# Attention into a mixture of experts on one core: first loads put on other queues and in another order, and one VectorE step ordered behind a copy

## The chip, the core and the metric

The kernel runs on one core of one Trainium2 chip. The metric is the device time of one launch in microseconds (us), as the median of several runs. A profile is one more execution, recorded instruction by instruction; its clock starts with the first instruction. Engines are written as the profile has them: PE (TensorE's matmuls) and PEld (its weight loads), DVE (VectorE), ACT (ScalarE), POOL (GpSimd) and SP (SyncE). A "q" behind a name (ACTq, SPq) marks work of that engine's sequencer, above all the issuing of DMAs.

## What is computed

Two stages follow each other. Attention has 8 batches, 8 heads, 576 positions and 64 values a head; heads 0 to 3 see a window of 32 positions, heads 4 to 7 every fourth position of a window of 128. Its output, 4608 rows of 512, goes into a layer of 8 experts, where each row is sent to the one expert with the highest score:

```python
scores = where(masks, q @ k.T / sqrt(D), -1e9)
attn = exp(scores - max); attn /= attn.sum() + 1e-9
x = (attn @ v) reshaped to (4608, 512)
expert = argmax(x @ w_gate); gate = softmax(x @ w_gate)[expert]
y = relu(x @ w1[expert]) @ w2[expert]        # 512 -> 1024 -> 512
out = gate * y
```

All is float32 outside; inside, only the masks are bf16.

## The kernel before, in words

**Attention** (`attention`, L487) is cut into 32 units: for each batch `b`, first the dilated heads (`ty` 1), then the plain ones (`ty` 0), each in two pairs of heads (`hl` 0 and 1). I number them u0 to u31. A unit goes through these steps, and the loop over `i` (L502) works on several units at once:

- `load_qk` (L265) and `load_v` (L289) bring q, k and v of one batch and type; each tile has one buffer, so that a load waits until the tile's last reader is through. For the first batch, `ty` 1 is loaded in two halves, one for each pair of heads.
- `turn` (L319) transposes q and k of a unit on PE (L338 for `ty` 0, L347 for `ty` 1). DVE copies q out of PSUM (L328) and ACT copies k (L330).
- `front` (L364) makes the scores on PE (L384). In batches 0 to 3 the mask is added on PE too (L372) and DVE finds the row maxima in PSUM (L400); later DVE adds the mask (L406) and then finds them (L413).
- `exponentials` (L417) runs ten ACT instructions, which also sum the rows into `den` (L421).
- `norm` (L431) belongs to the unit before: DVE adds a constant to `den` (L433), takes the reciprocal (L435), and POOL multiplies (L436).
- `weights` (L440), two steps behind, transposes on PE (L446); DVE copies (L448).
- `summed` (L452), three steps behind, multiplies by v (L461); ACT copies (L475, L482). `row_part` (L554) and `logit_part` (L570) make the rows for the experts and their scores.

When a batch is done, `route` (L583) and `tables` (L674) choose experts on DVE, POOL scatters the rows into a DRAM table `bucket` (L239), and the experts' slots become known.

**The experts** (`moe`, L1156) run in 35 or so slots of 128 rows. For each slot, `fetch` (L1132) loads the rows (L1087) and four weight blocks of 1 MB (L1106) on SP's queue. `across` (L1159) transposes the rows on PE (L1162), and DVE copies them to SBUF (L1164). Then come 64 matmuls for the first layer (L1230) and 16 for the second (L1262).

**What sets the order.** The program is written as one stream in which attention's steps and the slots' matmuls are interleaved by costs written into the code (`run_slots`, L1309). A scheduler then sets the order of instructions on each engine from readiness as it estimates it; on the chip each engine takes its instructions in that fixed order. `tc.issue_after(x)` makes an instruction stand behind `x`. The DMAs stand in the order of the queue that issues them.

At the start the queues hold this:

- SP: q of batch 0, `ty` 1 (8 DMAs, L283), q `ty` 0 (4, L270), v `ty` 1 (13, L308), v `ty` 0 (5, L292 and L295), the write of `blank` into `bucket` (L499), then q and k of batch 1, `ty` 1 (4 and 4, L278).
- ACT: the identity matrix (L186), k of batch 0, `ty` 1 (8, L283), k `ty` 0 (4, L270); behind these the ACT table load and the first copies of k.
- POOL: two mask tables (L208); after the first multiplication of `norm`, `w_gate` (L511), the packed constants `cst` (L514) and the third mask table; then `rows <- cst` (L559).

Of the kernel before, what the change touches and what calls it, by code (L numbers as in the profile page):

```python
# [16 lines left out]
OP = mybir.AluOpType  # L17
# [6 lines left out]
N, DM, E, F = B * S, H * DH, 8, 1024  # L24
# [11 lines left out]
CAP = N  # L36
# [23 lines left out]
NROWS = E * CAP + 128  # L60
# [103 lines left out]
def kernel(  # L164
# [10 lines left out]
    nc = tc.nc  # L175
    packed, at, exact, mask_at, packed_last, last_at = _constants()
    bucket = nc.dram_tensor("bucket", (NROWS, ROW), F32, kind="Internal").ap()
# [20 lines left out]
    blank = cpool.tile([128, ROW], F32, name="blank")  # L198
# [8 lines left out]
    def load_masks(i):  # L207
        nc.gpsimd.dma_start(masks[i], nc.inline_tensor(exact[i], name=f"c_mask{i}").ap())  # L208
# [11 lines left out]
    def wrote_bucket(i, b):  # L220


        i = getattr(i, "ins", i)
        tc.declare_no_dep(i, group="bucket", reason="no row is written twice")
        tc.add_to_no_dep_group("bucket", i)
        tc.declare_no_dep(i, group="reads", reason="rows read are full and not written again")
        bucket_writes.append((b, i))
# [22 lines left out]
    def bank(name, *dims):  # L250
        return psum.tile([128, *(dims or (512,))], F32, tag="bank", name=name)
# [5 lines left out]

    t, turns = {}, []  # L260


    STRIPS = ((0, 0, 0, 0, 96), (1, 0, 0, 96, 48), (1, 48, 1, 0, 48), (2, 0, 1, 48, 96))

    def load_qk(b, ty):  # L265
        for name, src, queue in (("q", q, nc.sync), ("k", k, nc.sync if b else nc.scalar)):
            if ty == 0:
                x = pool.tile([QT, S // QT, 4, DH], F32, tag=name + "0", name=f"{name}0_{b}", bufs=1)
                for h in range(4):
                    queue.dma_start(x[:, :, h, :], src[b, h].rearrange("(t p) d -> p t d", p=QT))  # L270
            else:


                x = pool.tile([96, 4, 3, 128], F32, tag=name + "1", name=f"{name}1_{b}", bufs=1)
                a = src[b, 4:8].rearrange("h (t m a) d -> m t h (a d)", m=2, a=2)
                for i, p0, m, t0, n in STRIPS:
                    if b:
                        queue.dma_start(x[p0 : p0 + n, :, i], a[m, t0 : t0 + n])  # L278

                for hl in () if b else range(2):  # L280
                    h = slice(2 * hl, 2 * hl + 2)
                    for i, p0, m, t0, n in STRIPS:
                        queue.dma_start(x[p0 : p0 + n, h, i], a[m, t0 : t0 + n, h])  # L283
            t[b, name, ty] = x

    def first_key(j):
        return max(0, 64 * j - WIN)

    def load_v(b, ty):  # L289
        if ty == 0:  # L290
            x = pool.tile([96, 4, 9, DH], F32, tag="v0", name=f"v0_{b}", bufs=1)
            nc.sync.dma_start(x[:, :, 0, :], v[b, 0:4, 0:96, :].rearrange("h p d -> p h d"))  # L292
            for h in range(4):
                a = v[b, h, 64 - WIN : 160 - WIN, :]
                nc.sync.dma_start(  # L295
                    x[:, h, 1:9, :],
                    bass.AP(a.tensor, a.offset, [[DH, 96], [64 * DH, 8], [1, DH]]),
                )
        else:
            x = pool.tile([96, 2, 9, 2 * DH], F32, tag="v1", name=f"v1_{b}", bufs=1)  # L300
            for j in range(9):
                lo, end = first_key(j), first_key(j) + 96
                while lo < end:
                    hi = min(end, (lo // STRIP + 1) * STRIP)
                    h, m, at0 = lo // (2 * STRIP), lo // STRIP % 2, lo % STRIP
                    a = v[b, 4 + h : 5 + h, DIL * at0 + 2 * m : DIL * at0 + 2 * m + 1, :]
                    p0 = lo - first_key(j)
                    nc.sync.dma_start(  # L308
                        x[p0 : p0 + hi - lo, :, j, :],
                        bass.AP(  # L310
                            a.tensor,
                            a.offset,
                            [[DIL * DH, hi - lo], [2 * S * DH, 2], [1, 2 * DH]],
                        ),
                    )
                    lo = hi
        t[b, "v", ty] = x
# [112 lines left out]

    def norm(e, den):  # L431

        nc.vector.tensor_scalar(den, den, 1e-9, None, op0=OP.add)  # L433
        rec = pool.tile([128, 9], F32, tag="rec", name="rec", bufs=3)
        nc.vector.reciprocal(rec, den)  # L435
        return nc.gpsimd.tensor_tensor(  # L436
            out=e, in0=e, in1=rec.unsqueeze(2).broadcast_to([128, 9, 96]), op=OP.mult
        )
# [48 lines left out]
    def attention():  # L487

        units = [(b, ty, hl) for b in range(B) for ty in (1, 0) for hl in range(2)]
        load_masks(0)
        for ty in (1, 0):
            load_qk(0, ty)
        load_masks(1)
        for ty in (1, 0):
            load_v(0, ty)

        wrote_bucket(nc.sync.dma_start(bucket[E * CAP : NROWS], blank), 0)  # L499
        qT = {n: turn(0, 1, 0, n) for n in "qk"}  # L500
        evs, dens, eTs, xTs = {}, {}, {}, {}
        for i in range(len(units) + LAG + 3):  # L502


            ended = None
            if 0 < i <= len(units):
                product = norm(evs[i - 1], dens.pop(i - 1))
                if i == 1:

                    with tc.issue_after(product.ins):  # L510
                        nc.gpsimd.dma_start(  # L511
                            wg[:, :, 0:E], moe_w_gate.rearrange("(c p) e -> p c e", p=128)
                        )
                        nc.gpsimd.dma_start(cst, nc.inline_tensor(packed, name="c_pack").ap())  # L514
                        load_masks(2)
            if i < len(units):
                evs[i], lo, places = front(qT["q"], qT["k"], units[i][1], units[i][0] < EARLY)
            u = i - LAG - 1
            if 0 <= u < len(units):
                b2, ty2, hl2 = units[u]  # L520
                xTs[u] = pool.tile([128, S], F32, tag="xT", name="xT", bufs=3)
                for part in range(2):
                    summed(eTs[u], b2, xTs[u], ty2, hl2, part)
                del eTs[u]
                if hl2 == 1 and b2 + 1 < B:
                    load_v(b2 + 1, ty2)
            if 0 <= u - 1 < len(units):
                b2, ty2, hl2 = units[u - 1]
                logit_part(b2, 2 * ty2 + hl2, xTs.pop(u - 1))
                ended = b2 if (ty2, hl2) == (0, 1) else None  # L530
            yield 3.0, ended

            if 0 <= i - LAG < len(units):
                eTs[i - LAG] = weights(evs.pop(i - LAG))
                yield 1.1, None
            if i + 1 < len(units):
                b2, ty2, hl2 = units[i + 1]
                qT = {}
                for n in "qk":
                    qT[n] = turn(b2, ty2, hl2, n)  # L540
                    yield 0.5, None
                if hl2 == 1 and b2 + 1 < B:
                    load_qk(b2 + 1, ty2)
            if 0 <= u < len(units):
                b2, ty2, hl2 = units[u]
                row_part(b2, 2 * ty2 + hl2, xTs[u])
                yield 0.55, None

            if i < len(units):
                dens[i] = exponentials(evs[i], lo, places)  # L550
# [19 lines left out]
    def logit_part(b, c, xT):  # L570


        for j, t0, n, at0 in [(j, TT * j, TT, 0) for j in range(NT - 1)] + [(0, S - REST, REST, TT)]:
            nc.tensor.matmul(  # L574
                logits[b][32 * j : 32 * j + 32, at0 : at0 + n],
                lhsT=wg[:, c],
                rhs=xT[:, t0 : t0 + n],

                start=c == 2 and at0 == 0,
                stop=c == 1 and (at0 > 0 or j > 0),  # L580
            )
# [529 lines left out]
    for j in range(NSLOT):  # L1111
        x = (j, "x", 0, 2 * j - 2)
# [43 lines left out]
    def moe():  # L1156


        def across(j):  # L1159
            ps = bank("xt", 4, 128)  # L1160
            for c in range(4):
                nc.tensor.transpose(ps[:, c], xs[j][:, 128 * c : 128 * c + 128], ident)  # L1162
            xt = mpool.tile([128, 4, 128], F32, tag="xt", name="xt")
            nc.vector.tensor_copy(xt, ps)  # L1164
            return xt

        late, xt = [], None
        for j in range(NSLOT):
# [11 lines left out]
            x = xs[j]  # L1180
            if xt is None:
                xt = across(j)
                yield 0.5
            h = mpool.tile([128, 8, 128], F32, tag="h", name="h")
# [108 lines left out]
            xt = nxt  # L1293
# [91 lines left out]
```

## Time and profile before

| What | Value |
|---|---|
| Median of 3 runs | 837.66 us (837.44 to 840.22) |
| The profiled execution: its own time | 781.94 us |
| The profiled execution: span from first to last instruction | 780.1 us |
| PE busy | 745.3 us, 96% of the span |
| PEld, DVE, ACT, POOL busy | 71%, 35%, 29%, 18% |
| Mean granted TensorE clock | 0.983 of full |
| Moved by DMA | 195.42 MB |

The profiled execution is shorter than the runs that are timed without a profile; a difference of two kernels is therefore worked out inside one profile and then set against the median. In a timeline each row is a start, a duration, an engine, a line, an operation, and the tiles (output, arrow, inputs); rows that follow each other on an engine are merged, and the bracket at the end tells how long the engine sat idle before and what ended that. In a table of windows, each row is a stretch of the span with the busy time of each engine, the granted TensorE clock and the DMA engines' share and rate. In a list of waits, each row names the waiting engine and line, what it waited for, the sum, the times, and the longest.

### The profile page before, as it was taken

The page shows a single profiled execution, that of the slowest core. Times are in us where ns is not written, and L with a number is a line of the kernel's source. Part 1 is how long each engine was busy: PE and PEld are TensorE (multiplying, and loading weights), DVE is VectorE, ACT ScalarE, POOL GpSimd, SP SyncE. Part 2 cuts the span into 40 slices and gives each one's busy share as a digit, 9 for nine tenths or more (in the row PEclk, how much of TensorE's full clock was granted, in tenths as well). Part 3 has the DMA queues.
Part 4 walks back from the last instruction along what each step waited for, and adds up shares of the span by engine and source line. Part 5 has one row for each costly group of instructions (what it writes and reads, how often), then busy time and mean ns, then how long its engine had stood idle before and what let it go on. Part 6 is the DMA issues. An engine that isn't in the chain of part 4 may idle for free.

```text
span 780.1 us, 18140 instructions
## 1 busy us (share of the span) xinstructions
PE 745.3 (96%) x6870; PEld 557.5 (71%) x6870; DVE 275.6 (35%) x963; ACT 228.9 (29%) x853; POOL 141.1 (18%) x134
## 2 busy tenths in 40 slices
PE   6798996999999999999999999999999999999993
PEld 4587875887777777777777776776776483686781
DVE  3567785755443433452241410280010111011010
ACT  3787874663333333223331100100100100100100
POOL 0414351313211310131110200160000000000000
PEclk9899998999999999999999999999999999999997
DMA  7965779999899998888317838999981683984996
GB/s 186 210 162 153 197 210 303 292 296 304 249 327 323 312 330 241 291 311 307 93 46 233 255 141 299 326 354 378 317 301 32 205 306 134 335 273 137 319 324 211
DMA packets 179644, 195.42 MB, mean 250 GB/s; under 512 B 73552, under 2 KB 105952, under 8 KB 179554
## 3 DMA queue, kind: packets, MB, share of 16 engines
q1 hardware_dynamic: 166960, 169.01, 68.8%
q0 software_dynamic: 6832, 20.54, 7.0%
q10 hardware_dynamic: 5762, 4.67, 2.0%
q8 instruction: 57, 0.93, 0.5%
q14 instruction: 33, 0.27, 0.1%
HBM read 216.16 MB, written 21.54 MB: 305 GB/s over the span
## 4 chain that ended last, share of the span: by engine, by line
PE 84%; ACT 5%; DVE 4%; issue 2%; DMA 2%; another core or an unknown queue 1%; SPq 0%; POOLq 0%; POOL 0%; ACTq 0%; DVEq 0%
PE ph L1230 32%; PE py L1262 29%; PE xo L461 4%; ACT e L421 4%; PE scores L384 3%; PE weights L446 3%; PE xt L1162 2%; PE ph L1192 2%; PE py L1192 2%; PE xrow L564 2%; PE turned L347 1%; PE turned L338 1%; PE logits L574 1%; DMA k<-in_k_dram 1%
## 5 line engine op out<-in xcount | busy, mean ns | idle before, releaser
L1230 PE MATMUL ph<-xt,w 128*128 128x128 f32 x2240 | 269.3, 276 | 4.9 <-DVE xt L1164 4.9
L1230 PEld LDWEIGHTS ph<-xt,w 128*128 128x128 f32 x2240 | 260.6, 192 | 18.6 <-issue 12.4
L1262 PE MATMUL py<-w,h 128*128 128x512 f32 x560 | 254.9, 596 | 0.0
L1262 PEld LDWEIGHTS py<-w,h 128*128 128x128 f32 x560 | 100.4, 190 | 98.1 <-issue 96.4
L1279 POOL DMA_INDIRECT out_dram<-y,to x35 | 34.7, 992 | 373.3 <-ACT y L1273 311.6
L1164 DVE COPY xt<-xt 128x512 f32<-128x512 f32 x38 | 26.2, 690 | 179.5 <-PE xt L1162 179.4
L1273 ACT ACTIVATE y<-py,x 128x512 f32<-128x512 f32 x35 | 24.0, 687 | 208.9 <-PE py L1262 161.7
L436 POOL TENSOR_TENSOR e<-e,rec 128x864 f32<-128x864 f32 x32 | 52.3, 1633 | 130.6 <-DVE rec L435 112.1
L448 DVE COPY eT<-weights 96x384 f32<-96x384 f32 x96 | 47.5, 545 | 33.0 <-PE weights L446 32.7
L421 ACT ACTIVATE e<-e,lo 128x96 f32<-128x96 f32 x144 | 51.8, 361 | 15.3 <-DVE lo L413 15.3
L421 ACT ACTIVATE e<-scores,lo 128x96 f32<-128x96 f32 (+1 forms) x160 | 52.6, 346 | 10.8 <-DVE lo L400 10.5
L239 POOL DMA_INDIRECT bucket<-rows,idx x40 | 39.1, 977 | 64.1 <-DVE idx L662 47.5
L1250 DVE TENSOR_SCALAR h<-ph 128x512 f32<-128x512 f32 x35 | 24.1, 689 | 71.4 <-PE ph L1230 71.3
L330 ACT COPY kT<-turned 128x288 f32<-128x288 f32 x64 | 22.5, 406 | 77.6 <-PE turned L338 40.3
L1241 ACT ACTIVATE h<-ph 128x512 f32<-128x512 f32 x35 | 20.8, 595 | 81.3 <-PE ph L1230 75.8
L461 PE MATMUL xo<-eT,v 96*64 96x64 f32 (+1 forms) x1216 | 44.3, 228 | 0.2 <-ACT kT L330 0.2
L461 PEld LDWEIGHTS xo<-eT,v 96*64 96x64 f32 x1216 | 39.8, 141 | 5.2 <-issue 1.1
L446 PE MATMUL weights<-ident,e 128*96 128x128 f32 x288 | 37.8, 277 | 1.8 <-POOL e L436 1.8
L384 PEld LDWEIGHTS scores<-kT,qT 64*64 64x64 f32 x1152 | 32.1, 143 | 10.0 <-issue 3.8
L384 PE MATMUL scores<-kT,qT 64*64 64x96 f32 x1152 | 37.5, 262 | 1.2 <-ACT kT L330 1.0
L446 PEld LDWEIGHTS weights<-ident,e 128*96 128x96 f32 x288 | 31.8, 128 | 8.2 <-issue 4.8
L421 ACT ACTIVATION_READ_ACCUMULATOR e<-scores,lo 128x1 f32 (+1 forms) x160 | 33.5, 210 | 0.0
(218 smaller groups left out, 592.0 us busy)
## 6 DMA issues: line engine op xcount, KB each, us to landing
w<-in_moe_w_dram SPq DMA_DIRECT2D x164, 1024.0 KB
x<-bucket SPq DMA_DIRECT2D x26, 257.0 KB
v<-in_v_dram SPq DMA_DIRECT2D x32, 192.0 KB
q<-in_q_dram SPq DMA_DIRECT2D x32, 144.0 KB
v<-in_v_dram SPq DMA_DIRECT2D x48, 96.0 KB
k<-in_k_dram SPq DMA_DIRECT2D x28, 144.0 KB
x<-bucket ACTq DMA_DIRECT2D x11, 257.0 KB
q<-in_q_dram SPq DMA_DIRECT2D x14, 192.0 KB
```

What stands on the lines that cost most here:

```text
L239: nc.gpsimd.indirect_dma_start(out=bucket, out_offset=bass.IndirectOffsetOnAxis(ap=idx, axis=0), in_=rows, in_offset=None, bounds_check=NR ...
L384: nc.tensor.matmul(sc[r][64 * c : 64 * c + 64, 96 * (i % 5) : 96 * (i % 5) + 96], lhsT=qT[rows, 64 * j : 64 * j + 64], rhs=kT[rows, first_ ...
L421: nc.scalar.activation(out=e[p0:p1, i], in_=s[:, 96 * (i - i0) : 96 * (i - i0) + 96], func=AF.Exp, bias=lo[p0:p1, i : i + 1], scale=-1.0, ...
L436: return nc.gpsimd.tensor_tensor(out=e, in0=e, in1=rec.unsqueeze(2).broadcast_to([128, 9, 96]), op=OP.mult)
L446: nc.tensor.transpose(tp[0:96, 128 * i : 128 * i + 128], e[:, a + i], ident)
L448: nc.vector.tensor_copy(eT, tp[0:96, 0:384])
L461: nc.tensor.matmul(xo[DH * h : DH * h + DH, at0 : at0 + nq], lhsT=vt[:, 2 * hl + r, j, :] if ty == 0 else vt[:, hl, j, DH * r : DH * r + D ...
L1164: nc.vector.tensor_copy(xt, ps)
L1192: nc.tensor.matmul(out[mine], lhsT=lhsT[:, mine], rhs=ws[:, (j + (g >= KIND[mixed[j]])) % 2, c, cols], start=c == 0, stop=c == n - 1,)
L1230: nc.tensor.matmul(ph[:, fi], lhsT=w1[:, c, 128 * f : 128 * f + 128], rhs=xt[:, c], start=c == 0, stop=c == 3,)
L1262: nc.tensor.matmul(py, lhsT=h[:, f], rhs=w2[:, f], start=f == 0, stop=f == 7)
L1279: i = nc.gpsimd.indirect_dma_start(out=out, out_offset=bass.IndirectOffsetOnAxis(ap=to, axis=0), in_=y, in_offset=None, bounds_check=N - 1 ...
```

## The change

Three things are changed.

First, of batch 0's k, ACT's queue keeps only the four DMAs of the first pair of heads (`ty` 1, `hl` 0). The other eight (four for the second pair, four for `ty` 0) are issued by POOL, between and behind the two mask tables.

Second, on SP's queue only v of `ty` 1 stays ahead of batch 1's q and k; v of `ty` 0 and the write of `blank` come behind these.

Third, `norm`'s first DVE instruction is ordered behind the latest copy `xt` of a slot's transposed rows that stands before it in the program. Before the first slot there is no such copy, so the order binds nothing there.

```diff
-        for name, src, queue in (("q", q, nc.sync), ("k", k, nc.sync if b else nc.scalar)):
+        for name, src in (("q", q), ("k", k)):
+            queue = nc.sync if b or name == "q" else nc.gpsimd
...
-                        queue.dma_start(x[p0 : p0 + n, h, i], a[m, t0 : t0 + n, h])
+                        (nc.scalar if (name, hl) == ("k", 0) else queue).dma_start(
+                            x[p0 : p0 + n, h, i], a[m, t0 : t0 + n, h]
+                        )
...
-        nc.vector.tensor_scalar(den, den, 1e-9, None, op0=OP.add)
+        with ExitStack() as order:
+            if crossed:
+                order.enter_context(tc.issue_after(crossed[-1].ins))
+            nc.vector.tensor_scalar(den, den, 1e-9, None, op0=OP.add)
...
         load_masks(0)
-        for ty in (1, 0):
-            load_qk(0, ty)
+        load_qk(0, 1)
         load_masks(1)
-        for ty in (1, 0):
-            load_v(0, ty)
-        wrote_bucket(nc.sync.dma_start(bucket[E * CAP : NROWS], blank), 0)
+        load_qk(0, 0)
+        load_v(0, 1)
         qT = {n: turn(0, 1, 0, n) for n in "qk"}
...
                 if hl2 == 1 and b2 + 1 < B:
                     load_qk(b2 + 1, ty2)
+                if i == 0:
+                    load_v(0, 0)
+                    wrote_bucket(nc.sync.dma_start(bucket[E * CAP : NROWS], blank), 0)
...
-            nc.vector.tensor_copy(xt, ps)
+            crossed.append(nc.vector.tensor_copy(xt, ps))
```

More of the change, by code (lines that the diff above doesn't have):

```diff
@@ L251, in bank @@
         return psum.tile([128, *(dims or (512,))], F32, tag="bank", name=name)
-    t, turns = {}, []
+    t, turns, crossed = {}, [], []
     STRIPS = ((0, 0, 0, 0, 96), (1, 0, 0, 96, 48), (1, 48, 1, 0, 48), (2, 0, 1, 48, 96))
     def load_qk(b, ty):
-        for name, src, queue in (("q", q, nc.sync), ("k", k, nc.sync if b else nc.scalar)):
+        for name, src in (("q", q), ("k", k)):
+            queue = nc.sync if b or name == "q" else nc.gpsimd
             if ty == 0:
```

## The prediction

> **What bounds the kernel now.** I read the page's busy shares first (PE 96%), then tables of windows, the list of PE's waits, and timelines of the two places where PE waits. The windows show where PE is not full: from 240 us to 760 us every stretch of 20 us has 20.00 us of PE, while the first 240 us hold 217.53, and nearly all that is missing lies before 130. So the end is set by how early PE becomes full, and only the first 130 us can give anything. PE's waits there, the three longest:
>
> ```profile
> PE turned L347 <- DMA q<-in_q_dram: 5.4, 3, 3.2
> PE ph L1230 <- DVE xt L1164: 4.9, 1, 4.9
> PE turned L347 <- ACT xT L482: 2.5, 2, 1.9
> ```
>
> The first row is loads of q: 3.2 us before the first at the start, 0.4 in the start's further loads, 1.8 for batch 1. The second is one wait in front of the first slot. The start, from its timeline:
>
> ```profile
> 1.16 6.82 ACTq L283 DMA_DIRECT2D k<-in_k_dram  x8
> 8.17 2.43 ACTq L270 DMA_DIRECT2D k<-in_k_dram  x4
> 10.62 1.28 ACT L330 ACT_TABLE_LOAD   x1 [10.62 <-DMA k<-in_k_dram]
> 11.92 1.31 ACT L330 COPY kT<-turned 128x288 f32<-128x288 f32 x4
> 12.37 1.71 PE L384 MATMUL scores<-kT,qT 64*64 64x96 f32 x34
> 22.70 2.68 SPq L278 DMA_DIRECT2D q<-in_q_dram  x4
> ```
>
> ACT issues 12 loads of k until 10.60; only then come its table load, the copies of k, and the first scores at 12.37. The last row: batch 1's q is issued at 22.70, behind v. What this costs stands in the windows (stretch, its length, busy time of PE, PEld, DVE, ACT, POOL, PE clock, DMA share, GB/s):
>
> ```profile
> 30.00:32.00 2.00, 0.32 (x4) 0.32 (x4) 1.42 (x3) 2.00 (x14) 0.38 (x1) 1.00 1.09 217
> ...
> 34.00:36.00 2.00, 2.00 (x16) 0.96 (x18) 0.39 (x2) 0.70 (x4) 0.59 (x1) 0.50 1.08 244
> 36.00:38.00 2.00, 2.00 (x28) 1.62 (x24) 0.00 (x0) 0.97 (x3) 1.04 (x1) 0.50 0.47 107
> 38.00:40.00 2.00, 2.00 (x42) 1.69 (x40) 0.02 (x1) 0.38 (x1) 0.00 (x0) 0.50 0.04 8
> ```
>
> PE stands almost still at 30 to 32, with the DMA engines full, and then runs six us at clock 0.50. The first slot, from its timeline:
>
> ```profile
> 123.80 1.05 DVE L413 TENSOR_REDUCE lo<-e 128x9 f32<-128x864 f32 x1
> 123.96 0.66 PE L1162 MATMUL xt<-ident,x 128*128 128x128 f32 x4
> 128.31 0.17 DVE L433 TENSOR_SCALAR den<-den 128x9 f32<-128x9 f32 x1 [3.46 <-ACT e L421]
> 128.76 0.69 DVE L1164 COPY xt<-xt 128x512 f32<-128x512 f32 x1
> 129.51 2.08 PE L1230 MATMUL ph<-xt,w 128*128 128x128 f32 x8 [4.89 <-DVE xt L1164]
> ```
>
> PE has turned the rows by 124.62, but DVE's copy stands behind `den`, which waits for ten exponentials until 128.31. PE idles 4.89 us.
>
> **What the Trainium skill says.** "DMA: Bandwidth & Descriptors", section "Issuing engines are not separate DMA queues": loads from SP, ACT and POOL share the same 16 engines, so another queue saves only the time of issuing. The trace agrees that this time is not small here: 6.82/8 = 0.85 us for each on ACT. "TensorE: Matmul & The Clock Gate", Part 1: after an idle window of about 3.4 us PE falls to half clock, and needs about as long of work to come back. The trace agrees in kind: 0.50 after each of the pauses at 30 and 125 us, though the first was only 1.8 us in one piece. Same page, "Architectural detail": matmuls, ACT and DVE keep strict order. The rows above show it (a ready copy behind a waiting `den`).
>
> **The change, part by part.**
>
> *ACT's queue.* Eight of its 12 issues go: 4 x 0.85 + 2.43 = 5.8 us, so ACT is free at about 4.8 and its table loaded at 6.1. That is then hidden; q is late next. SP's issues do not change, and PE waited for their data at 10.05. In the changed program as built, PE turns the first half of the second pair's k and all its q before the first scores. Scores then start at about 10.05 (q) + 0.8 (last turns) = 10.9 for 12.37: 1.5 us gained. At most it is 12.37 - 9.3 = 3.1 (first pair's k turned at 8.9, then a copy), at least below zero if POOL's k lands late.
>
> *POOL's queue.* It gets eight issues. Plain loads take 0.55 (cst) to 0.81 us (`w_gate`, 512 pieces of 32 bytes) in the trace; k's have 96 to 576 pieces. I take 0.6 for the first four, 0.85 for the last four, as `w_gate`'s row is nearest: masks until 1.9, k's half until 4.3, masks until 5.0, the rest until 8.4. Landing took 4.65 us for the first mask table (1.23 to 5.88), so the half lands near 9 and the rest near 13. Needed are they at 10.5 and, for u2's turns, at about 14.5 (16.7 before): hidden by 1.5 us each. Behind these issues on POOL stands u0's multiplication, at 19.12 before, so nothing waits. Without the cover each late us costs one, since k's copies stand in ACT's order ahead of the exponentials. Bounds: -0.5 (less in ACT's way) to +4 us; I take 0.
>
> *SP's order.* SP ends v of `ty` 1 at 19.0; batch 1's q is then issued at 19.1 to 21.8 and its k until 24.7, 3.6 us earlier, and 5 v loads and `blank` (0.86 + 0.26 MB, some 4.5 us at 250 GB/s) no longer lie ahead in the DMA engines. The last q was issued at about 24.7 and landed at 31.68. I expect 21.8 + 3 = 25 for q (the start's last q, issued until 7.66, was there at 10.05, 2.4 us later) and 27.5 for k. PE will want them about 27. So the pause at 30 goes, and the half clock behind it. Its worth is read from the scores of u3, u4, u5, u6, which start at 25.13, 38.09, 44.23, 50.01: gaps of 12.96, 6.14, 5.78. With 6 to 6.2 for the first gap, 6.8 us are gained. The loads put back: v of `ty` 0 is issued until 27.5 and read first by u2's sums (45.20 before, some 36 after), `blank` is read by nobody early. Batch 1's `ty` 0, SP's next, comes at 34.6 for 35.1 and is needed near 39, landing near 37.6: cover of 1 to 2 us. If it is gone, up to 2 us return.
>
> *POOL's order, a by-product.* Before, `rows <- cst` waited for cst 3.7 us at 22.6 to 26.3 ahead of u1's multiplication; it then ran beside DVE's `den` of u2, which took 1.59 us for 0.17, and u3's maxima came 2.4 us after their scores. In the built order u1's multiplication is ahead of `rows <- cst`. Gain between 0 and 2.4; I take 1.
>
> *PE's order.* In batches 2 and 3 the built order puts 15 of a unit's 20 sums ahead of the scores (batch 1 had that before, and no longer has). 0.75 x 1.36 = 1.0 us, twice, with ACT waiting behind: I take -1.8 of 0 to -2.
>
> Sum of the start: 1.5 + 0 + 6.8 + 1 - 1.8 = 7.5. From u4 to the first slot the units are bound by PE and ACT together, 5.9 us each, with loads ahead of them, so the shift is carried.
>
> *The tie.* `den` stands behind the copy. Queued behind both are later units' DVE steps; whoever waits for `norm` is POOL, then `weights` one unit later. The copy can start when L413 ends, 124.85, plus about 0.1, so PE starts at 125.65 for 129.51: 3.86 us. Weights blocks are issued from 116.58; 1 MB at the 390 GB/s of this stretch is 2.7 us, so the first is there by about 121. Next on PE come `weights` for a unit multiplied at 114.83 to 116.46: ready. PE's work at clock 0.50 between 129.5 and 132.5 loses 1.5 us; with a pause of 1 us for 4.9 about half is saved, 0.7. Sum 4.5. In later slots the copy stalled nobody, and a late `norm` has cover: the unit with `den` at 245.75 was multiplied until 247.98, its `weights` came at 272.52.
>
> Total 7.5 + 4.5 = 12.0: the profiled execution goes from 781.94 to 769.9 (span 768.1). The timed runs are 56 us longer around the same program; I take the difference over unchanged: 837.66 - 12.0 = 825.7.
>
> **The rivals.**
> - *A, forecast*: 825.7, own range 822 to 829. Chance 0.56.
> - *B, the first slot finds its weights late.* The wait for the copy becomes one for w. For: four blocks share engines at full load until 128.6. Against: they stand in order. 837.66 - 7.5 = 830.2; 0.14.
> - *C, the start's gain is hidden anyway*, as the DMA engines (share over 1 at 20 to 32) deliver no sooner in total. Against: at 16 to 20 the share is 0.36 to 0.42. Only the tie is left: 833.2; 0.11.
> - *D, more than forecast*: the half clock at 70 to 74 (about 2 us) goes too, and the reordered sums cost nothing (1.8): 821.9; 0.10.
> - *E, nothing shows*: the shift is lost at the routing of batches 0 and 1, where DVE and POOL set the pace, and the slot wait moves: about 837; 0.05.
> - *F, slower: POOL's descriptors.* Place: the eight k loads ahead of the first scores. If each takes t us, the last lands at 1.9 + 9t + 3, free up to t = 1.07. The 12 us are eaten at t = 2.4; beyond it every 0.1 costs 0.9. With t = 3.0 it is 837.66 - 12 + 17.4 = 843. The trace's 0.81 speaks against it; 0.04.
>
> **How the numbers follow.** About 0.5% (4.2 us) is what a measurement of this kernel can tell from no change. Faster than 833.5: A, B, D and half of C, 0.86. Within: half of C, E, 0.10. Slower: F, 0.04. A, B and D hold 0.80: range 820.0 to 832.5, which takes in D with a margin of 2 us for its clock, and B with the POOL bound.
>
> **What would show it.** First scores at 10.5 to 11.5, u4's near 29 to 30, no clock of 0.50 between 28 and 42; `xt` copied before `den` at the first slot, 7 to 9 us earlier than 128.76 plus 4; PE full from about 118. Wrong would be: turns of k waiting for POOL's loads; L347 waiting for q or k at 27; L1230 waiting for w; `weights` L446 waiting for POOL's multiplication after 130.

## The result, and the profile after

| | before | after |
|---|---|---|
| median of 6 runs each, us | 837.76 (836.05 to 842.60) | 830.15 (828.26 to 830.38) |
| ratio, 95% interval | | 0.9893 (0.9866 to 0.9920) |
| profiled execution, its own time / span, us | 781.94 / 780.1 | 830.33 / 828.5 |
| mean granted TensorE clock | 0.983 | 0.956 |

The ratio, which is not that of the two medians, makes 9.0 us less, with an interval of 6.7 to 11.2. The medians lie 7.6 us apart, within that interval; the forecast was 12.0 less. The change makes the kernel faster, on the side and by the two means that the prediction named, but its sum is 3.0 us too large by the ratio and 4.4 by the medians.

The spans of the two profiles can't be set against each other: in some sessions on the chip every execution of either kernel has pauses of about 6 us whenever GpSimd scatters a batch's rows, in others none has, so that one kernel takes 837 us or 783, and times are compared below only within a session. The first profile of before has no pauses, the profile of after has them. A second profile of before, with pauses, is the first experiment; ahead of the first scatter, at 72 us, the two profiles of before agree within 0.6 us.

Now the lines that answer to those of before. PE's waits (engine, line, what it waited for: sum, times, longest) of after:

```profile
PE turned L351 <- DMA q<-in_q_dram: 3.8, 3, 3.3
PE turned L342 <- ACT xT L483: 2.4, 1, 2.4
...
PE ph L1239 <- DVE xt L1173: 1.0, 1, 1.0
```

The wait in front of the first slot is 1.0 us instead of 4.9, and of the waits for q the start's first 3.3 us are left and little else. The start, from the timeline of after:

```profile
1.16 2.05 ACTq L285 DMA_DIRECT2D k<-in_k_dram  x4
1.95 2.46 POOL L285 DMA_DIRECT2D k<-in_k_dram  x4
3.24 1.28 ACT L334 ACT_TABLE_LOAD   x1 [3.24 <-DMA ident<-c_id]
...
8.90 0.70 ACT L334 COPY kT<-turned 128x288 f32<-128x288 f32 x2 [4.38 <-PE turned L351]
...
11.51 1.86 PE L388 MATMUL scores<-kT,qT 64*64 64x96 f32 x36
...
14.08 0.40 ACT L334 COPY kT<-turned 128x288 f32<-128x288 f32 x1 [3.76 <-PE turned L351]
...
19.09 1.88 SPq L280 DMA_DIRECT2D q<-in_q_dram  x4
```

ScalarE has issued its k by 3.21 and its table is there at 4.52, both 1.6 us sooner than predicted (4.8 and 6.1): the first four issues take 2.05 us, 0.51 each, where the prediction took 0.85, the mean of eight. GpSimd's first four issues cost 2.46/4 = 0.61 us each, where 0.6 was assumed. Batch 1's q goes out at 19.09 instead of 22.70. What this does to PE stands in the windows of after (stretch, length, busy time of PE, PEld, DVE, ACT, POOL, clock, DMA share, GB/s):

```profile
30.00:32.00 2.00, 2.00 (x57) 1.58 (x55) 0.39 (x2) 1.99 (x9) 0.00 (x0) 1.00 1.10 148
...
34.00:36.00 2.00, 1.88 (x19) 1.61 (x18) 1.97 (x6) 2.00 (x13) 0.55 (x1) 1.00 0.96 207
36.00:38.00 2.00, 2.00 (x47) 1.50 (x44) 0.58 (x2) 1.99 (x10) 0.00 (x0) 1.00 1.00 226
38.00:40.00 2.00, 2.00 (x50) 1.83 (x50) 1.49 (x6) 1.24 (x6) 0.95 (x1) 1.00 0.95 227
```

At 30 to 32 PE is full, where it had 0.32 us of work, and from 34 to 40 the clock stays at 1.00 where it was 0.50. The first slot, from the timeline of after:

```profile
129.52 1.05 DVE L417 TENSOR_REDUCE lo<-e 128x9 f32<-128x864 f32 x1
129.68 0.66 PE L1171 MATMUL xt<-ident,x 128*128 128x128 f32 x4
130.61 0.69 DVE L1173 COPY xt<-xt 128x512 f32<-128x512 f32 x1
131.35 1.16 PE L1239 MATMUL ph<-xt,w 128*128 128x128 f32 x8 [1.02 <-DVE xt L1173]
```

The copy follows the maxima (they end at 130.57) at once; no `den` stands between.

To see where time went I set the starts of the same work against each other, kernel by kernel: the first score matmul of each unit, the first `ph` and `py` of each half slot. The **lead** is how much sooner after reaches a point. Each is read from two single executions, and early in the program these differ by some 0.5 us of themselves. Whole executions differ by more: the timed ones of before in the session of runs 5 to 8 go from 777.9 to 786.9 us, so a lead holds for the two executions that it was read from, and the timed runs tell what is usual.

### The profile page after: what moved, and what is told of

Its sections match the earlier page's. It is cut to its first block, busy times and chain, and to the rows that moved or that the text cites. A ratio compares the mean times of both kernels' runs of the same rounds, so it can differ in the third digit from the quotient of the medians.

```text
span 828.5 us, 18147 instructions
## 1 busy us (share of the span) xinstructions
PE 773.6 (93%) x6870; PEld 574.1 (69%) x6870; DVE 274.4 (33%) x963; ACT 229.1 (28%) x853; POOL 146.3 (18%) x142
## 4 chain that ended last, share of the span: by engine, by line
PE 85%; issue 5%; ACT 5%; DVE 1%; another core or an unknown queue 1%; DMA 1%; POOLq 0%; ACTq 0%; POOL 0%; DVEq 0%
PE ph L1239 31%; PE py L1271 29%; PE xo L469 5%; PE weights L454 3%; PE scores L388 3%; ACT e L425 3%; PE turned L342 2%; PE xt L1171 2%; PE ph L1201 2%; PE py L1201 2%; PE logits L583 2%; PE xrow L573 2%; PE turned L351 2%; DMA k<-in_k_dram 1%
## 5 line engine op out<-in xcount | busy, mean ns | idle before, releaser
L1239 PE MATMUL ph<-xt,w 128*128 128x128 f32 x2240 | 276.4, 280 | 4.1 <-issue 3.1
L1239 PEld LDWEIGHTS ph<-xt,w 128*128 128x128 f32 x2240 | 267.3, 196 | 18.0 <-issue 15.7
L1271 PE MATMUL py<-w,h 128*128 128x512 f32 x560 | 262.5, 609 | 3.9 <-issue 3.9
L1271 PEld LDWEIGHTS py<-w,h 128*128 128x128 f32 x560 | 102.8, 194 | 107.9 <-issue 105.9
L469 PE MATMUL xo<-eT,v 96*64 96x64 f32 (+1 forms) x1216 | 51.6, 233 | 13.7 <-issue 13.6
L469 PEld LDWEIGHTS xo<-eT,v 96*64 96x64 f32 x1216 | 44.1, 144 | 21.0 <-issue 16.6
L454 PEld LDWEIGHTS weights<-ident,e 128*96 128x96 f32 x288 | 32.2, 129 | 10.4 <-issue 8.1
L410 DVE TENSOR_TENSOR e<-scores,masks 128x384 f32<-128x384 f32 x64 | 23.0, 399 | 33.7 <-PE scores L388 18.1
```

The lines of the kernel that those rows point to most:

```text
L454: nc.tensor.transpose(tp[0:96, 128 * i : 128 * i + 128], e[:, a + i], ident)
L469: nc.tensor.matmul(xo[DH * h : DH * h + DH, at0 : at0 + nq], lhsT=vt[:, 2 * hl + r, j, :] if ty == 0 else vt[:, hl, j, DH * r : DH * r + D ...
L1239: nc.tensor.matmul(ph[:, fi], lhsT=w1[:, c, 128 * f : 128 * f + 128], rhs=xt[:, c], start=c == 0, stop=c == 3,)
L1271: nc.tensor.matmul(py, lhsT=h[:, f], rhs=w2[:, f], start=f == 0, stop=f == 7)
```

## The experiments

The queues and the tie in the change are independent edits, so the first four runs take them apart in one session (before: 837.12 us, 48 runs). Theories: mine, that the start gives 7.5 us and the tie 4.5; rivals, that one of them gives all of it, or that part of it is lost behind.

**1. Before, once more.** No edit.

> The kernel before, unchanged, for a second profile: its first was 781.94 us with a span of 780.1 at a clock of 0.983, while its timed runs are near 837. Theory: the 56 us don't lie around the program, as the prediction had it, but inside it, and a usual execution has them as pauses at the routing of each batch, when GpSimd scatters rows, as the profile after the change shows them: span 834 to 839, clock near 0.955, and TensorE idle 5 to 7 us in each of some eight such places. Rival: the time around the program is really longer for this kernel: span near 780 again, and a time near 837 if the execution is a timed one.

Measured: 839.24 us, span 837.5, clock 0.947. The 56 us lie inside the program, as the theory says. A pause, from this profile's timeline, during the five scatters of batch 0:

```profile
73.85 0.32 PE L461 MATMUL xo<-eT,v 96*64 96x64 f32 x2 [0.16 <-issue]
73.91 1.01 POOL L239 DMA_INDIRECT bucket<-rows,idx  x1 [0.30 <-issue]
74.58 0.36 PE L461 MATMUL xo<-eT,v 96*64 96x64 f32 x4 [0.41 <-issue]
75.22 0.97 POOL L239 DMA_INDIRECT bucket<-rows,idx  x1 [0.30 <-issue]
75.36 0.31 PE L461 MATMUL xo<-eT,v 96*64 96x64 f32 x3 [0.42 <-issue]
76.11 0.48 PE L461 MATMUL xo<-eT,v 96*64 96x64 f32 x3 [0.43 <-issue]
...
79.81 0.42 ACT L475 COPY xT<-xo 128x320 f32<-128x320 f32 x1 [6.99 <-remote]
```

PE gets two to four matmuls every 0.75 us and waits for nothing that the profile can name ("issue"); ScalarE stands for 6.99 us; GpSimd goes on, a scatter every 1.3 us, and here so does SP, with seven loads issued from 73.62 to 76.97. From u9's to u10's scores it takes 13.7 us, 7.1 in the first profile. There are eight such places, behind most of them the clock is at 0.50 for some 7 us, and they stand alike in the profile of after. So the prediction's reading of the 56 us as something around the program falls.

With this trace the lead of after is 7.5 us at u4's scores, 5.7 at u16's, 9.6 at the first `ph`, 11.1 at u17's scores, 10.5 behind the second slot, and 9.0 at the end.

**2. The tie alone.** Before, with

```diff
+            if crossed:
+                order.enter_context(tc.issue_after(crossed[-1].ins))
             nc.vector.tensor_scalar(den, den, 1e-9, None, op0=OP.add)
...
-            nc.vector.tensor_copy(xt, ps)
+            crossed.append(nc.vector.tensor_copy(xt, ps))
```

> The kernel before with the tie alone (the first VectorE instruction of the division is issued after the copy of the slot's turned rows). My theory, as predicted: -4.5 us (3.9 at the first expert slot, some 0.7 more by the clock), so a ratio of 0.9945. Rival, that the start alone makes the 9 us: 0 to -1 us, ratio 0.999 to 1.000, although the wait of the first ph for xt falls from 4.9 to 1.0 us, because the experts' stage then waits elsewhere.

Measured: 831.16 us (22 runs), ratio 0.9931 (0.9906 to 0.9955): -5.8 us, -3.8 to -7.9. From u16's scores to the first `ph` it takes 5.2 us for 9.1, and from u16's to u17's scores 11.3 for 16.6. The rival falls: what the tie wins is not lost again further on.

**3. The start alone.** After, with

```diff
-            if crossed:
+            if False:
```

> The kernel after without the tie: new queues and new order of the first loads, the old order on VectorE. My theory, as predicted: -7.5 us, ratio 0.991; the trace: first scores at 11.5, the fourth unit at 30.4 instead of 38, no clock of 0.50 between 28 and 42, and the first ph waits near 4 us for xt. Rival, that what is won at the start is mostly lost behind it (the batch 0 routing and the pauses there are reached earlier, and the attention of batch 1 waits for other loads): -3 to -5 us, ratio 0.994 to 0.996.

Measured: 830.79 us (11 runs), ratio 0.9928 (0.9905 to 0.9952): -6.0 us, -4.0 to -8.0. Scores of u0 at 11.03, of u4 at 29.82; the wait for `xt` is 4.9 us. That is between the two theories (-7.5, and -3 to -5), and the interval doesn't decide between them. Both parts are real: -6.0 and -5.8.

**4. SP's order alone.** Before, with v `ty` 0 and `blank` behind batch 1's q and k, and k on ScalarE's queue as before:

```diff
-        for ty in (1, 0):
-            load_v(0, ty)
-        wrote_bucket(nc.sync.dma_start(bucket[E * CAP : NROWS], blank), 0)
+        load_v(0, 1)
...
+                if i == 0:
+                    load_v(0, 0)
+                    wrote_bucket(nc.sync.dma_start(bucket[E * CAP : NROWS], blank), 0)
```

> The kernel before with the order on the SP queue alone (v of type 0 and the blank rows behind q and k of batch 1); k stays on the ACT queue. My theory: -6.8 us of the start's 7.5, ratio 0.992, the fourth unit's scores at 31 to 32 and the first at 12.4 as before. Rival, that the ACT queue's twelve issues ahead of the first copies are the larger part: -2 to -4 us.

Measured: 833.07 us (22 runs), ratio 0.9960 (0.9943 to 0.9978): -3.3 us, -1.8 to -4.8, where 6.8 was forecast. The number is the rival's, but its reason isn't borne out: run 6 puts k's queue alone at -2.0. Why SP's order alone gives less is seen in PE's and POOL's rows of this run's timeline:

```profile
26.37 0.44 POOL L559 TENSOR_SCALAR rows<-cst 128x5 f32<-128x5 f32 x2 [4.41 <-DVE den L433]
26.78 3.21 POOL L436 TENSOR_TENSOR e<-e,rec 128x864 f32<-128x864 f32 x2
28.45 1.58 PE L446 MATMUL weights<-ident,e 128*96 128x128 f32 x9 [1.75 <-POOL e L436]
29.83 1.17 PE L347 MATMUL turned<-ident,q 96*128 96x96 f32 x6
```

Batch 1's q is there at 29.83, so the loads are in time as forecast. But u1's multiplication still stands behind `rows <- cst`, PE waits 1.75 us for it, and runs at half clock from 30 to 32. The gap from u3's to u4's scores is 8.5 us; in the whole change 5.6, in before 13.0. The by-product on POOL's queue, which the prediction put at 1 us, is worth the other 2.8 of the gap, by the difference to the whole change; the sixth run comes to it from the other side.

The second session had no pauses (before: 782.94 us, 53 runs).

**5. The whole change.** No edit.

> The whole change once more, beside its parts on one chip. If the parts add up: -6.0 (start alone) and -5.8 (tie alone) make -11.8 us, ratio 0.986. Rival: the parts overlap, the whole stays at -8 to -9.5 us, ratio 0.989 to 0.990, because what is won ahead of the first expert slot is partly given back in the pauses behind it.

Measured: 776.39 us (9 runs), ratio 0.9922 (0.9891 to 0.9954): -6.1 us, -3.6 to -8.5. Neither expectation was met: the parts, which were measured in the session with pauses, don't add up here, and the whole falls short of the rival's 8, which its interval just takes in. Its trace (span 774.0) can be set against the first profile of before (780.1). The lead is 7.9 us at u4's scores, 6.4 at u16's, 10.3 at the first `ph`, and 11.7 from u17's scores on, in this execution within 0.3 of the forecast of 12.0 (the ninth run shows less). Then 4.9 us go in one place, and 6.8 remain to the last matmul (the tail behind the last scatter differs by another 0.7). The place, from the timeline of this run:

```profile
146.37 13.07 SPq L299 DMA_DIRECT2D v<-in_v_dram  x4
160.46 1.55 SPq L1096 DMA_DIRECT2D x<-bucket  x2
163.78 1.08 PE L1171 MATMUL xt<-ident,x 128*128 128x128 f32 x4 [3.55 <-DMA x<-bucket]
164.66 4.65 PE L1239 MATMUL ph<-xt,w 128*128 128x128 f32 x32
```

PE wants the rows of slot 2 (counted from 0) at 160.2. SP issues their read only at 160.46, since it has spent 13 us on four loads of v of batch 4, and they land 3.3 us later. PE idles 3.55, and the 32 matmuls behind, which begin at half clock, take 4.65 us instead of 3.74. The same work in the first profile of before:

```profile
163.14 1.55 SPq L1087 DMA_DIRECT2D x<-bucket  x2
171.88 0.66 PE L1162 MATMUL xt<-ident,x 128*128 128x128 f32 x4
```

The read was issued at 163.14 and wanted at 171.88: 8.7 us, of which the landing needs 3.3, so 5.4 us of room. PE came 11.7 us sooner and SP 2.7: 9.0 - 5.4 = 3.6 us too late, the 3.55 of the row.

**6. The queue of k alone.** Before, with k on GpSimd's queue but for one pair, and the second masks between:

```diff
-        for name, src, queue in (("q", q, nc.sync), ("k", k, nc.sync if b else nc.scalar)):
+        for name, src in (("q", q), ("k", k)):
+            queue = nc.sync if b or name == "q" else nc.gpsimd
```

> The kernel before with the queue of k alone: twelve of the sixteen strips of k and the second masks on GpSimd's queue, the order on SP's queue as before. My theory, as predicted: -1.5 us (first scores near 11), ratio 0.998, the fourth unit's scores still near 37 because k of batch 1 stands behind v and the blank rows. Rival, that the ACT queue's part is the larger, since the start alone gave 6.0 and SP's order alone 3.3: -2.7 us, ratio 0.997, by an earlier landing of everything behind it.

Measured: 780.27 us (22 runs), ratio 0.9975 (0.9958 to 0.9992): -2.0 us, -0.6 to -3.3. Between the two. First scores at 10.49; u1's multiplication on POOL is at 21.55 here, ahead of `rows <- cst`, so this edit, and not SP's order, brings the by-product; u4's scores are at 33.9, 4 us sooner than in before. With the fourth run this explains the start: the gap from u3's to u4's scores is 10.3 us here, 2.7 less than in the first profile of before, and SP's order alone took 4.5 off it. Each half leaves the other's wait in the gap, and together they make the 7.3 of the whole change: in this gap the two add up.

**7 and 8. The scatters spread out,** on after and on before. Each of a batch's five scatters (thirteen at the end) gets its own copy of its indices, issued some 3 us of work apart:

```diff
-            to_bucket(idx[0:n, i : i + 1], row[0:n, i], b)
+            pending.append((dest[0:n, i : i + 1], row[0:n, i], b))
...
+            with tc.issue_after(seen[-1].ins):
+                nc.vector.tensor_copy(idx, dest)
+            to_bucket(idx, row, b)
```

> The kernel after with one edit: the scatters of a batch's rows into the bucket are no longer issued five (at the end thirteen) in a row; each has its own copy of its indices on VectorE, some 3 us of work apart. Batch 0's five still come together, as a control. Theory of the pauses: TensorE, VectorE, ScalarE and SP starve when scatters follow each other at 1.3 us, and not at single ones (those of the output, some 15 to 20 us apart, show no gaps): the pauses of batches 2 to 7 and of the last thirteen shrink to under 2 us each, the span falls from 828 to 790 to 805, and batch 0's pause stays at 5 to 7 us. Rival, that each scatter costs its share wherever it stands: 826 to 832, with as much idle TensorE time, spread.

> The kernel before with the same edit to the scatters, so that the change can be read with few pauses behind it. If the pauses take back a part of the gain, the change is worth 11 to 12.5 us here (this kernel less the one of the run above); rival: 8 to 9.5 us as with the pauses. Its own time by the theory of the pauses: 800 to 817; by the rival: 835 to 840.

Measured: 776.69 us (21 runs), ratio 0.9928 (0.9907 to 0.9948), and 783.96 (14 runs), ratio 1.0025 (0.9997 to 1.0054). There were no pauses to remove, so nothing follows on their cause. But the trace of run 7 shows the wait of the fifth run again: the rows of slot 2 are asked for at 161.27, behind the same loads of v, PE waits 2.60 us for them, and the lead falls from 10.5 to 6.2 us. With the spread, the change is worth 783.96 - 776.69 = 7.3 us by the medians, which can't be told from the 6.1 above.

The third session had none either (before: 782.48 us, 36 runs).

**9. The whole change again,** the partner of the next run.

> The whole change again, as the partner of the run after it. One chip so far shows pauses at the scatters in all its runs (before 837, after 830), another shows next to none (783 and 776.4). On a chip with pauses: ratio 0.987 to 0.990, and the second expert slot's rows wait for nothing. On one without: ratio 0.992, the lead is 11.7 us up to the scores of the batches behind the first slot and 6.8 us behind the wait of the third slot's transposes for its rows.

Measured: 775.69 us (17 runs), ratio 0.9924 (0.9903 to 0.9945): -6.0 us, as in the fifth run. But in the execution that was profiled (span 771.7) the wait is not there:

```profile
158.30 1.55 SPq L1096 DMA_DIRECT2D x<-bucket  x2
...
162.36 0.65 PE L1171 MATMUL xt<-ident,x 128*128 128x128 f32 x4
```

SP was 2.2 us sooner and PE 2.1 later than in the fifth run, and the lead of 9.5 us holds from u17's scores through the slots. So my expectation of the trace failed: the room for the rows is about nothing, met in one execution and missed in another. This one, with 773.48 us, was the second fastest of its 17 (773.47 to 779.09), so it is not the usual case. It also shows that the wait is not all that is missing: the lead behind the tie is 9.5 and not 11.7, since the start gave 5.9 at u16 and PE ran at half clock for 3.4 us behind the first slot's wait of 1.0 us, which it did not in the fifth run.

**10. The rows of slots 2 and 3 by ScalarE's queue.** After, with

```diff
-            queue = nc.sync
+            queue = nc.scalar if j in (2, 3) else nc.sync
```

> The kernel after with one edit: the rows of expert slots 2 and 3 are read from the bucket through ScalarE's DMA queue, no longer through SP's, where they stand behind v of the fourth batch. Theory (on a chip without pauses the lead of 11.7 us is cut to 6.8 by the transposes of slot 2, which wait 3.55 us for these rows, and by half a clock after it): 4 to 5 us less than the run above there, the wait for the rows gone and the lead near 11 us to the end. On a chip with pauses there is no such wait: 0 to -1 us. Rival: the DMA engines are full (share 1.03 at 150 to 160), so the rows or the weights behind them land no sooner, and the loss comes one or two slots later: 0 to -1.5 us on either chip.

(The v in question is that of batch 4, counted from 0.) Measured: 773.87 us (8 runs), ratio 0.9900 (0.9868 to 0.9932). By the medians that is 1.8 us less than the run above, which the intervals don't tell apart. No transposes of a slot wait for rows. But PE waits for weights, 1.0 us before slot 1, 0.4 and 1.7 us later, and the lead falls from 10.5 to 5.8 us in pieces. SP took 16.7 us for v of batch 4, `ty` 1, in this execution. This speaks for the rival: the rows come in time, and the weights pay. It is one execution, and the second slowest of its eight (772.19 to 777.37), so a hint and no more. The statement of the Trainium skill that the prediction drew on ("DMA: Bandwidth & Descriptors", section "Issuing engines are not separate DMA queues") says the same: a queue more is no engine more.

**Spread, again** (run 11).

> The scatters spread, as before, in case this chip shows the pauses. Theory: with pauses, those of batches 2 to 7 and of the last thirteen scatters fall to under 2 us each and that of batch 0 stays, so 25 to 40 us less than the whole change above. Rival: each scatter costs its share wherever it stands: within 3 us of it. On a chip without pauses it says nothing (within 1 us, as measured).

Measured: 777.19 us (18 runs), ratio 0.9942 (0.9920 to 0.9964). No pauses here either; nothing follows on them. The wait for the rows of slot 2 is there once more, 2.45 us, and the lead falls from 9.2 to 5.3. So three of the four traces without pauses in which v stands ahead of these rows on SP's queue show it (runs 5, 7 and 11, not run 9).

**12. v of batch 4 later on SP's queue.** After, with

```diff
-                if hl2 == 1 and b2 + 1 < B:
+                if hl2 == 1 and b2 + 1 < B and (b2, ty2) != (3, 0):
                     load_v(b2 + 1, ty2)
+                if (b2, ty2, hl2) == (4, 1, 0):
+                    load_v(b2, 0)
```

> The kernel after with one edit: the five loads of v of type 0 of batch 4 (counted from 0) are issued on SP's queue one unit later, behind the rows of expert slots 2 and 3, the weights behind these and q and k of batch 5; in the kernel after they are issued from 146.4 to 159.4 ahead of those rows. No transfer is added, left out or put on another queue. Theory, that the order on SP's queue is what holds the rows of slot 2: on a chip without pauses the wait of 3.55 us and the half clock behind it are gone, no weight comes later, and the ratio to before is 0.987 to 0.989 (the whole change alone: 0.992). Rival, that the DMA engines are full there and any order loses as much: 0.991 to 0.993. On a chip with pauses: as the whole change, 0.987 to 0.990.

Measured, in a session without pauses (before: 779.47 us, 11 runs): 771.82 us (6 runs), ratio 0.9877 (0.9839 to 0.9915): -9.6 us, -6.6 to -12.5. Its timeline:

```profile
144.50 4.02 SPq L1098 DMA_DIRECT2D x<-bucket  x2
150.08 3.99 SPq L1117 DMA_DIRECT2D w<-in_moe_w_dram  x3
154.12 12.48 SPq L272 DMA_DIRECT2D q<-in_q_dram  x4
161.37 0.66 PE L1173 MATMUL xt<-ident,x 128*128 128x128 f32 x4
161.86 3.74 PE L1241 MATMUL ph<-xt,w 128*128 128x128 f32 x32
```

The rows are asked for 16 us sooner, the weights behind them 13 us sooner, and now it is q that takes SP 12.5 us. PE waits for none of these, and the lead of 10.5 us before slot 1 is 9.9 behind slot 2 and stays there to the last matmul. My theory holds: the order in SP's queue decides. The ratio lies in the range that it gave. Its interval overlaps with those of the whole change (0.9922, 0.9924), but each of its six executions (769.13 to 773.08) is faster than each of the 26 of runs 5 and 9 (773.35 to 779.09), while the fastest ones of before are alike in the three sessions (777.9, 777.5, 778.0). So this version is very likely faster than after; a session with both in it was not run. It is faster than before beyond doubt.

## Why the prediction was right in part

| step | forecast, us | measured, us |
|---|---|---|
| ScalarE's queue: first scores | 1.5 | 0.9 against the first profile, 0.3 against the second; at u3 0.6 (run 5), 0.2 (run 9) or -0.2 (after against run 1) are left |
| GpSimd's queue | 0 | not seen apart; its first issues take 0.61 each |
| SP's order and POOL's by-product: the gap from u3 to u4 | 6.8 + 1 | 7.3 to 7.7; of it 2.7 to 2.8 by POOL's order |
| PE's order in batches 2 and 3 | -1.8 | -1.2 (run 5) and -1.4 (run 9), from u10's to u16's scores |
| the start at u16 | 7.5 | 6.4 (run 5), 5.9 (run 9), 6.7 (run 12); against run 1: 5.7 (after), 7.0 (run 3); alone -6.0 |
| the tie: first `ph` sooner | 3.86 | 3.88 in each pair of traces |
| the tie: clock behind it | 0.7 | 1.4 (runs 2, 5, 7 and after), -0.1 to -0.25 (runs 9 to 12) |
| lead behind both | 12.0 | 11.7 (run 5), 9.5 (run 9), 10.5 (run 12), 11.1 (after against run 1) |
| the end | 12.0 | 9.0; without pauses 6.1 and 6.0 |

**What held.** The copy of the rows is the clearest: the time at which it could start was read off the line ahead of `den`, and 3.88 us came for 3.86. The clock behind it comes in two sizes: 1.4 us where PE stays at full clock behind the first slot, and about -0.2 where it falls to half, in four traces each; the forecast of 0.7 lies between them and was met by neither. The start came out 0.5 to 1.8 us short of its 7.5, and was wrong in its shares. SP's order alone gives a gap of 8.5 and not 6 to 6.2, because the by-product on POOL's queue was put at 1 and is some 2.8; the multiplication behind `rows <- cst` was seen, but not that PE's `weights` would wait for it as soon as the loads no longer hid it. The signs that the prediction set (first scores at 10.5 to 11.5, u4's near 30, no half clock from 28 to 42) came, the first at its edge (11.51). "PE full from about 118" can't be read in a profile with pauses; in run 5 PE is full from 119.2 on, but for the wait at slot 2.

**What failed: the step from the lead to the total.** "Total 7.5 + 4.5 = 12.0" takes the lead at the first slot to the end unchanged. The prediction looked for what is late next in front of that slot alone, at its weights (rival B), and they were in time. It didn't follow the queue of SP to the slots behind. Without pauses that is shown: PE is 11.7 us sooner at slot 2, SP 2.7, the room was 5.4, and the rows come too late by 3.55 us (run 5); runs 7 and 11 have the same wait, with 2.60 and 2.45 us, and lose 4.3 and 3.9 us of lead at it, run 5 4.9. With the loads of v put behind the rows it is gone (run 12). In the profile of before this could have been read: the read's issue at 163.14, its use at 171.88. The rest of the shortfall lies ahead of it: the start, the copy and the clock behind it gave 9.5 to 11.7 us together, and not 12.0.

With pauses, as in the result, it is another story. There PE in the profile of after waits for no rows of a slot. Its lead against run 1 is 10.4 us through the slots' middle, 13.1 when the last thirteen scatters begin, and 9.0 behind them, where after loses 4.05 us. This part changes from execution to execution: the same stretch costs the tie alone 0.93 us and the start alone 0.88 against run 1. That the pauses as such take back 3 us of the 12 is therefore not shown. Nor is it certain that something is missing: the parts sum to -11.8 with some 2 us of uncertainty each, and the whole is -9.0 with 2.2.

**The other reason that fell** is "56 us longer around the same program". They are pauses inside it. Taking the difference over unchanged was good luck in its size, since the profile that it was taken from had no pauses, and the runs had.

Rival B named a time, 830.2, that agrees with the result, but its mechanism (the first slot's weights) appears in no trace. C and E are out by runs 2 and 3, F by the 0.61 us of an issue. Of D, the half clock at 70 to 74 is gone in runs 5, 9 and 12, but the reordered sums cost 1.2 to 1.4 us, and the result lies 8 us above 821.9.

## What to carry to other kernels

When PE is moved forward, follow each queue past the place of the edit and list, for each tile that PE will want, when its load is issued and when it is used: such a difference, less the time that the load takes to land, is the room there. What PE gains beyond the room and beyond what the issue itself gains is lost again at that tile, however well the edit itself was sized. When two waits lie in one gap, measure each edit alone too: here the sum of the gap was right and the shares were not. And before a profile is set against medians, see that its span is that of the runs; if not, look for the difference inside the program, where it lay here.

## What the runs showed of the hardware that was not expected

**Pauses beside rows of scatters.** Where GpSimd scatters rows five or thirteen times in a row, 1.3 us apart, TensorE gets a few instructions every 0.7 to 1.3 us, and ScalarE none for up to 7.2 us (run 1). VectorE and SP stand in some of these places (8.05 us of VectorE and 11.6 us of SP at the last row of run 1) and go on in others, as SP does at the first row. By their times, every execution of the session of the result and of that of runs 1 to 4 has the pauses, and none of runs 5 to 12. The first profile of before has none, though the runs that stand beside it took 837 us; the record doesn't say whether it was taken in their session. The window of 540 to 560 us of after (columns as above):

```profile
540.00:560.00 20.00, 13.02 (x64) 8.52 (x63) 6.69 (x47) 0.60 (x1) 12.65 (x14) 0.76 0.73 230
```

Without pauses, with the same thirteen scatters from 505.7 on, the first profile of before has

```profile
500.00:520.00 20.00, 20.00 (x113) 14.26 (x113) 13.52 (x94) 1.97 (x3) 11.88 (x13) 1.00 1.00 328
```

The single scatters of the output, 14 to 26 us apart, show no gap except close behind such a row, and from batch 3 on three to five scatters of a row are issued before TensorE's first gap (runs 1 and after). The packets that bring instructions are no slower (median of the 57 on queue q8: 960 ns in the first profile of before, 958 in run 1, 961 in after). What it is, and why a session has it or not, stays open; the record gives the same chip number for runs 1 to 4, which have it, and for run 12, which hasn't. The test by spreading the scatters met no session with pauses.

**The half clock comes after short waits, too, and not each time.** In front of the first slot PE waits 1.01 to 1.03 us for `xt` in after and in runs 2, 5, 7 and 9 to 12. In after and runs 2, 5 and 7 the clock stays at 1.00 behind it; in runs 9 to 12 it is at 0.50 for 3.4 us. From the windows of run 9:

```profile
118.00:120.00 2.00, 0.97 (x12) 0.69 (x7) 1.65 (x2) 0.95 (x5) 0.00 (x0) 1.00 1.05 408
120.00:122.00 2.00, 2.00 (x12) 1.96 (x12) 0.00 (x0) 2.00 (x13) 0.00 (x0) 0.56 1.04 368
```

The prediction went by an idle window of about 3.4 us. Here the clock fell at 120.2, and in the 3.4 us ahead of that PE waited 0.77 and 1.02 us and worked for the rest; so less than such a window was enough. What tells the two cases apart was not tested. At slot 2 of run 5 the wait was longer, 3.55 us, and the clock fell:

```profile
162.00:164.00 2.00, 0.22 (x1) 0.25 (x2) 0.00 (x0) 1.71 (x10) 0.00 (x0) 0.79 0.80 223
164.00:166.00 2.00, 2.00 (x11) 2.00 (x11) 0.98 (x3) 0.00 (x0) 0.00 (x0) 0.50 0.60 138
```

Run 4 fell to 0.50 from 30 to 32 after a stretch (26 to 28) with 0.71 us of work in 2 and a wait of 1.75 us. In run 5 the wait of 3.55 us cost 4.9 in all.
